# Transposes that load 104 stationary columns, and 104 partitions behind them, in a fused RWKV-7 and gated-cosine kernel

## The chip, the cores and the metric

The kernel runs on one core of a Trainium2 chip. The metric is the device time of one execution in microseconds (us); with one core, that core is the slowest. A profile shows one execution; the median is over several others.

The core's engines are TensorE (PE, with its weight loads listed apart as PEld), VectorE (DVE), ScalarE (ACT) and GpSimd (POOL). SyncE (SP) issues most of the DMAs. A matmul has two operands: the stationary one, which a weight load puts into the array, and the moving one, which streams past it. The stationary operand's columns become the output's partitions, the moving operand's columns become the output's columns.

## The reference

An attention block of the RWKV-7 kind runs a recurrence over 768 steps for 4 batches and 8 heads with head size 40. Its output feeds a feed-forward block with a cosine gate.

```python
for t in range(S):                                       # S = 768; r, k, v, w, a, b: (4, 8, 768, 40)
    y[:, :, t] = np.einsum('bhd,bhde->bhe', rt, state)
    Sa = np.einsum('bhde,bhe->bhd', state, at)
    state_decay = state * wt[:, :, None, :] - np.einsum('bhd,bhe->bhde', Sa, bt)
    state = state_decay + np.einsum('bhd,bhe->bhde', vt, kt)
x = y.transpose(0, 2, 1, 3).reshape(3072, 320)
h = x @ w_in                                             # w_in: (320, 2048)
out = (h * np.cos(h)) @ w_out                            # w_out: (2048, 320)
```

## The kernel before

**Tiling.** The sequence is cut into 24 chunks of C = 32 steps. A chunk of the 4 batches fills 128 partitions, as (batch, step). The 8 heads lie along the free dimension, each padded from D = 40 to DP = 64 columns, in tiles such as `nat`, `vp`, `rp`, `bn` and `kn`.

**Transposes.** Products within a chunk need head dimensions on partitions. `turned` (line 323) makes four transposes of a tile: each takes two neighbouring heads, 2 x 64 = 128 columns, as the stationary operand and the 128 x 128 identity as the moving one. In the result, partitions 0 to 39 hold the first head of the pair, 64 to 103 the second; 40 to 63 and 104 to 127 hold padding. `half` (line 76) names the two slices of 40 partitions that the later matmuls read. `full` (line 77) names the two halves of 64.

`turned` is called for the decays (`p1_w`), for a (`p1_a`), for b divided by a decay (`p1_b`), for v and r (`p2_v`) and for k (`p2_k`). Two places transpose on their own: `p1_a` turns the running decay products `wb` back to (batch, step) partitions for the first four chunks (line 415), and `ch_t` turns the state, eight transposes a chunk (line 558). After each group, ScalarE or VectorE copies the result out of PSUM. One PSUM tile of `at` is two banks, 2 x 512 columns of 128 partitions.

**What follows a transpose.** `p1_w` makes `wb`, the running products of decays within the chunk, by a scan on VectorE (chunks 0 to 3) or by a plain copy on ScalarE. `wc` keeps the last product of each chunk, and GpSimd sets the first one to 1 (`from_one`). `a_W` multiplies the turned a by `wb`. `p2_g`, `ch_q`, `ch_x` and `ch_s` are groups of small matmuls of 32 or 40 rows and columns. `ch_z` (line 629) accumulates the state's change in `dps`. It first zeroes whole halves of 64 partitions with a matmul of zeros. Then VectorE adds the change to the state `qz` (line 656), GpSimd multiplies the state by the chunk's decay `wc` (line 657), VectorE makes the outputs `yt` (line 663), and GpSimd scales these by `wb` (line 668). `tokens` sends two slices of 40 partitions of `yt` to DRAM and reads them back as `xT`.

**The feed-forward block.** It is cut into pieces: `first_a` and `first_b` make `ph` from `xT` and `w_in`, ScalarE and VectorE make the cosine gate, `second` makes `po`. `mm` (line 100) issues every matmul that isn't a transpose, so line 101 stands for all of them.

**Order.** The whole order is written out by hand: the scheduler is off, and for each chunk a list of segments (lines 919 to 994) says which piece of the recurrence and which piece of the feed-forward block comes next. Work that must come some steps later is put off with `later`. Each engine works through its list in this order. `busy` and `shifted` put extra matmuls of zeros at a few places.

Of the kernel before, what the change touches and what calls it, by code (L numbers as in the profile page):

```python
# [12 lines left out]
ALU = mybir.AluOpType  # L13
# [7 lines left out]
def kernel(  # L21
# [43 lines left out]
    nc = tc.nc  # L65
    B, H, S, D = r.shape
    P, C, DP = 128, 32, 64
# [4 lines left out]
    N72 = C + D  # L72
# [3 lines left out]
    half = [slice(DP * e, DP * e + D) for e in range(2)]  # L76
    full = [slice(DP * e, DP * e + DP) for e in range(2)]
    every = slice(0, P)

    const = ctx.enter_context(tc.tile_pool(name="const", bufs=1))  # L80
    ring = ctx.enter_context(tc.tile_pool(name="ring", bufs=7))
# [8 lines left out]
    def kept(name, shape, n=1, fill=None, part=lambda t: t, on=nc.gpsimd):  # L90

        tiles = []
        for i in range(n):
            t = const.tile(shape, F32, tag=f"{name}{i}", name=f"{name}{i}")
            if fill is not None:
                on.memset(part(t), fill)
            tiles.append(t)
        return tiles
# [4 lines left out]
    def pick(t, offset, *dims):  # L103

        return bass.AP(t.tensor, t.offset + offset, [list(t.ap[0]), *(list(d) for d in dims)])
# [8 lines left out]
    ident = kept("ident", [P, P])[0]  # L114
# [5 lines left out]
    for n, fill in (("w", 1.0), ("a", 0.0), ("b", 0.0)):  # L120
        for i in range(4):
            x = slice((i - 2) * H * DP, (i - 1) * H * DP)
            if i < 2:
                t = const.tile([P, H, DP], F32, tag=f"nat_{n}{i}", name=f"nat_{n}{i}")
            else:
                t = {
                    "w": w_in_sb[:, 0, late:], "a": w_in_sb[:, 1, late:], "b": late_out
                }[n][:, x].rearrange("p (h d) -> p h d", h=H)
# [4 lines left out]
    for n in "kvr":  # L133
        t = const.tile([P, H, D], F32, tag=f"nat_{n}", name=f"nat_{n}")
# [8 lines left out]
    NZ = 2 * (C + DP) - DP + D  # L143
    qz = kept("qz", [P, B, 2, NZ], 1, 0.0, on=nc.vector)[0]
# [178 lines left out]
    def turned(ps, x):  # L323

        for i in range(4):
            nc.tensor.transpose(  # L326
                ps[:, i * P : (i + 1) * P], x[:, 2 * i : 2 * i + 2].rearrange("p e d -> p (e d)"), ident
            )

    flat = lambda t: t.rearrange("p q t -> p (q t)")  # L330
    b4 = lambda t: t.rearrange("p (q t) -> p q t", t=C)
    unpad = lambda t: t[:, :, :D]
    G = {"rest": []}
# [24 lines left out]
    def p1_w(c):  # L358
        ps = at("wT")
        for i in range(2):  # L360
            turned(ps[:, i], nat["w", c + i])
        if c < 4:

            for i in range(2):
                nc.scalar.copy(G["w1"][:, i, :, 0:1], b4(ps[:, i])[:, :, 0:1])
            nc.vector.memset(ps[:, :, ::C], 0.0)
        for i in range(2):
            wb = ring.tile([P, 4 * P + 1], F32, tag="wb", name="wb")
            if c < 4:
                nc.vector.tensor_tensor_scan(  # L370
                    wb[:, 1:], ps[:, i], flat(G["w1"][:, i]), 0.0, ALU.mult, ALU.add
                )
            else:
                nc.scalar.copy(wb[:, 1:], ps[:, i])
            wc = ring.tile([P, 4 * B], F32, tag="wc", name="wc")
            nc.gpsimd.tensor_copy(wc, wb[:, C::C])
            G["wb", c + i], G["wx", c + i], G["wc", c + i] = wb, b4(wb[:, : 4 * P]), wc
            if c >= 4:
                from_one(c + i)
        if c == 8:  # L380
            later(2, lambda: over_w(c, unpad(nat["w", c])))
        elif c >= 4:
            over_w(c, unpad(nat["w", c]))

    def from_one(c):

        nc.gpsimd.memset(G["wb", c][:, : 4 * P : C], 1.0)

    def over_w(c, wn):
        rw = ring.tile([P, H, D], F32, tag="rw", name="rw")  # L390
# [4 lines left out]
    def a_W(c, aps):  # L395
        aT = ring.tile([P, 4, P], F32, tag="aT", name="aT")
        nc.vector.tensor_tensor(
            aT.rearrange("p j (b t) -> p (j b) t", b=B), b4(aps), G["wx", c], ALU.mult
        )
        G["aT", c] = aT  # L400

    def p1_a(c):
        if c >= 4:
            ps = at("aps")
            for i in range(2):
                turned(ps[:, i], nat["a", c + i])
            for i in range(2):
                a_W(c + i, ps[:, i])
            over_w(c + 1, unpad(nat["w", c + 1]))
            return  # L410
        for c in range(c, c + 2):
            wn = ps_h.tile([P, 512], F32, tag="h", name="wn")
            aps = ps_o.tile([P, 512], F32, tag="o", name="aps")
            for j in range(4):
                nc.tensor.transpose(
                    wn[:, j * P : (j + 1) * P], G["wb", c][:, j * P + 1 : (j + 1) * P + 1], ident
                )
            from_one(c)
            turned(aps, nat["a", c])
            over_w(c, unpad(wn.rearrange("p (h d) -> p h d", h=H)))  # L420
            a_W(c, aps)

    def p1_b(c):
        ps = at("bT")
        for i in range(2):
            turned(ps[:, i], bn_b[(c + i) % 7])
        for i in range(2):
            bT = sb3.tile([P, 4, P], F32, tag="opT", name="bT")
            nc.scalar.copy(bT.rearrange("p j t -> p (j t)"), ps[:, i])
            G["bT", c + i] = bT  # L430

    def p1_n(c):
# [75 lines left out]
    def p2_v(c):  # L508
        ps = at("vT")
        turned(ps[:, 0], vp)  # L510
        turned(ps[:, 1], rp)
        G["vT"] = sb3.tile([P, 4, P], F32, tag="opT", name="vT")
        G["rT", c] = sb2.tile([P, 4, P], F32, tag="rT", name="rT")
        nc.scalar.copy(G["vT"].rearrange("p j t -> p (j t)"), ps[:, 0])
        nc.scalar.copy(G["rT", c].rearrange("p j t -> p (j t)"), ps[:, 1])

    def p2_k(c):
        ps = at("kT")
        turned(ps[:, 0], kn_b[c % 2])
        G["kT"] = sb3.tile([P, 4, P], F32, tag="opT", name="kT")  # L520
        nc.scalar.copy(G["kT"].rearrange("p j t -> p (j t)"), ps[:, 0])

    def p2_g(c):
        kT, vT, aT, rT = G["kT"], G["vT"], G["aT", c], G["rT", c]
# [29 lines left out]
    def ch_t(c):  # L554
        ps = at("sT")
        G["s"] = sb1.tile([P, 2 * B, P], F32, tag="s", name="s")
        for i in range(2 * B):
            nc.tensor.transpose(  # L558
                ps[:, i // 4, (i % 4) * P : (i % 4 + 1) * P], qz[:, i // 2, i % 2, C : C + P], ident
            )  # L560
        for i in range(2):
            nc.scalar.copy(G["s"][:, 4 * i : 4 * i + 4].rearrange("p i e -> p (i e)"), ps[:, i])  # L562

    def ch_q(c):
        ps = at("qps")
# [63 lines left out]
    def ch_z(c):  # L629
        ps = [at("dps") for _ in range(2)]  # L630
        sm = G["sm"]

        for bb in range(B):
            for e in range(2):
                mm(
                    ps[bb // 2][full[e], bb % 2, : 4 * N72], idle[blk[bb], :DP],
                    pick(idle[blk[bb]], 0, (0, 4), (1, N72)), True,
                )
        for s, n in ((0, kn_b[c % 2]), (1, bn_b[c % 7])):
            for j in range(4):  # L640
                o = C - C * (j // 2)
                for bb in range(B):
                    for e in range(2):
                        mm(
                            ps[bb // 2][half[e], bb % 2, j * N72 : (j + 1) * N72],
                            n[blk[bb], 2 * j + e, :D],
                            sm[e][blk[bb], j, :] if s else vvm[c % 2][blk[bb], 2 * j + e, o : o + N72],
                            False,
                        )
        wx, wc = G["wx", c], G["wc", c]  # L650
        yt = sb1.tile([P, 4, B, C], F32, tag="yt", name="yt")
        for bb in range(B):
            dp = ps[bb // 2][:, bb % 2]
            if c < NCH - 1:
                z = pick(qz[:, bb], C, (DP, 2), (NZ, 2), (1, D))
                nc.vector.tensor_tensor(z, pick(dp, 0, (2 * N72 + C, 2), (N72, 2), (1, D)), z, ALU.add)  # L656
                nc.gpsimd.tensor_tensor(  # L657
                    z, z,
                    wc.rearrange("p (f m b) -> p f m b", f=2, m=2)[:, :, :, bb]
                    .unsqueeze(3).to_broadcast([P, 2, 2, D]),  # L660
                    ALU.mult,
                )
            nc.vector.tensor_tensor(  # L663
                yt.rearrange("p (f m) b t -> p f m b t", f=2)[:, :, :, bb],
                pick(dp, D, (2 * N72 - D, 2), (N72, 2), (1, C)),
                pick(qz[:, bb], 0, (NZ - C, 2), (NZ, 2), (1, C)), ALU.add,
            )
        nc.gpsimd.tensor_tensor(  # L668
            yt.rearrange("p j b t -> p (j b) t"), yt.rearrange("p j b t -> p (j b) t"), wx, ALU.mult
        )  # L670
        later(2, lambda: tokens(c, yt))

# [158 lines left out]
    with tc.manual_schedule():  # L831
# [88 lines left out]
        for c in range(NCH):  # L920
            t, q, x, s, z = main(c)
# [109 lines left out]
```

## Time and profile before

| | |
|---|---|
| runs before, us | 825.33, 826.02, 822.83; median 825.33 |
| the profiled execution, span from first to last instruction | 823.7 us; the profile gives no other time for it |
| mean granted TensorE clock | 0.948 of full |
| TensorE busy from 240 to 760 us | 515.25 of 520.00 us, clock 1.00 |
| TensorE busy from 0 to 62 us | 31.88 us, clock 0.76 |
| transposes of line 326: matmuls, weight loads | 88.13 us, 70.53 us, 576 of each |
| transposes of line 558: matmuls, weight loads | 26.4 us, 21.7 us, 184 of each |
| transposes of line 415: matmuls, weight loads | 4.3 us, 3.2 us, 16 of each |

Busy times of matmuls and loads overlap, with each other and among themselves: a matmul is counted from its start to its modelled end, and the next may start before that. So a mean duration isn't the distance from one matmul to the next; the distance comes from how long a group of several takes. A group's row in the profile gives line, engine, operation, output<-inputs, shapes, count, busy us, mean ns of one, and the engine's idle time before it with what ended it. A shape such as 128*128 128x320 is the rows and columns of the stationary operand, then those of the moving one.

### The profile page before, as it was taken

What the parts mean: (1) busy time and instruction counts of PE and PEld (TensorE: products, weight loads), DVE (VectorE), ACT (ScalarE), POOL (GpSimd) and SP (SyncE); (2) the same over time, 40 slices, a digit from 0 to 9 for tenths busy, and PEclk for the clock granted to TensorE, in tenths of its full rate; (3) what the DMA queues carried; (4) which work ended last, traced back from release to release, by engine and by line L of the source; (5) the groups of instructions that cost most, each with busy time, mean ns of one, the idle gap of its engine ahead of it and who ended that gap; (6) DMA issues with size and microseconds to landing.
All of it is one profiled execution on the core that took longest, in us unless ns stands there. A gap on an engine that the chain in (4) does not pass through costs nothing.

```text
span 823.7 us, 37673 instructions
## 1 busy us (share of the span) xinstructions
PE 746.9 (91%) x16832; PEld 571.3 (69%) x16832; DVE 509.3 (62%) x1081; ACT 383.8 (47%) x707; POOL 201.3 (24%) x352
## 2 busy tenths in 40 slices
PE   3656778899689999999999999999999999999997
PEld 2534456677467777778777777777787777777775
DVE  6987887859645599354797553895444874332231
ACT  1214676544244553545446446435635445363352
POOL 5315554430214023212221230330330222201000
PEclk9757799899789999999999999999999999999999
DMA  8456663244043322333223323214310212101000
GB/s 120 78 132 168 173 162 104 46 119 69 25 98 84 64 59 52 69 100 65 54 37 71 68 63 67 61 37 65 66 41 24 45 35 52 21 21 37 20 17 16
DMA packets 183297, 55.66 MB, mean 68 GB/s; under 512 B 157152, under 2 KB 178656, under 8 KB 183136
## 3 DMA queue, kind: packets, MB, share of 16 engines
q1 hardware_dynamic: 180560, 51.95, 29.2%
q8 instruction: 132, 2.16, 1.1%
q10 hardware_dynamic: 2320, 0.98, 0.6%
q0 software_dynamic: 256, 0.33, 0.2%
q14 instruction: 29, 0.24, 0.1%
HBM read 42.07 MB, written 11.14 MB: 65 GB/s over the span
## 4 chain that ended last, share of the span: by engine, by line
PE 63%; DVE 19%; ACT 6%; DMA 4%; issue 3%; SPq 3%; POOL 1%; DVEq 0%; ACTq 0%; POOLq 0%
PE ph L101 22%; PE po L101 20%; DVE inv_tmp L468 4%; DVE inv L472 4%; PE x0ps L101 3%; PE dps L101 3%; SPq L152 3%; PE gram L101 2%; DVE rw L391 2%; PE vT L326 2%; PE sps L101 2%; PE qps L101 1%; DVE turns L732 1%; PE nps L101 1%; PE sT L558 1%
## 5 line engine op out<-in xcount | busy, mean ns | idle before, releaser
L101 PE MATMUL po<-w_out_sb,gT 128*128 128x320 f32 x768 | 227.0, 445 | 0.0
L101 PE MATMUL ph<-xT,w_in_sb 128*128 128x256 f32 x768 | 189.5, 393 | 4.8 <-DVE gT L740 3.8
L101 PEld LDWEIGHTS po<-w_out_sb,gT 128*128 128x128 f32 x768 | 142.4, 193 | 55.9 <-issue 4.2
L101 PEld LDWEIGHTS ph<-xT,w_in_sb 128*128 128x128 f32 x768 | 142.3, 194 | 33.9 <-issue 13.9
L730 ACT ACTIVATE turns<-ph,rnd 128x512 f32<-128x512 f32 x96 | 63.8, 685 | 157.2 <-PE ph L101 156.7
L732 DVE SCALAR_TENSOR_TENSOR turns<-turns,ph 128x512 f32<-128x512 f32 x96 | 63.8, 684 | 109.2 <-ACT turns L730 108.9
L740 DVE TENSOR_TENSOR gT<-ph,turns 128x512 f32<-128x512 f32 x96 | 65.6, 685 | 36.3 <-ACT turns L737 36.3
L657 POOL TENSOR_TENSOR qz<-qz,wc 128x160 f32<-128x160 f32 x92 | 43.2, 489 | 163.1 <-DVE qz L656 162.6
L472 DVE TENSOR_TENSOR inv<-inv,inv_tmp 128x31 f32<-128x31 f32 (+15 forms) x186 | 72.0, 387 | 6.4
L468 DVE TENSOR_TENSOR inv_tmp<-u,inv 128x31 f32<-128x31 f32 (+15 forms) x186 | 70.0, 376 | 4.4
L736 ACT ACTIVATE turns<-turns 128x512 f32<-128x512 f32 x96 | 60.2, 627 | 23.3 <-DVE turns L732 23.3
L737 ACT ACTIVATE turns<-turns,half_pi 128x512 f32<-128x512 f32 x96 | 69.3, 722 | 3.1
L490 POOL COPY vp<-nat_v 128x320 f32<-128x320 f32 x25 | 12.5, 501 | 182.9 <-DMA nat_v<-in_v_dram 144.1
L101 PE MATMUL ph<-xT,w_in_tail 64*128 64x256 f32 x384 | 54.8, 404 | 0.0
L656 DVE TENSOR_TENSOR qz<-dps,qz 128x160 f32<-128x160 f32 x92 | 28.9, 315 | 33.9 <-PE dps L101 33.8
L391 DVE RECIPROCAL rw<-nat_w 128x320 f32<-128x320 f32 x20 | 42.8, 2142 | 0.1
L562 ACT COPY s<-sT 128x512 f32<-128x512 f32 x46 | 24.5, 584 | 37.6 <-PE sT L558 37.6
L101 PEld LDWEIGHTS ph<-xT,w_in_tail 64*128 64x128 f32 x384 | 33.3, 187 | 10.4 <-issue 6.6
L668 POOL TENSOR_TENSOR yt<-yt,wb 128x512 f32<-128x512 f32 x24 | 31.3, 1306 | 22.4 <-DVE yt L663 22.4
L546 ACT COPY vvm<-gram 128x256 f32<-128x256 f32 x24 | 8.8, 368 | 55.6 <-DVE ag L541 55.3
L101 PEld LDWEIGHTS sps<-x,rt 32*32 32x32 f32 x1536 | 18.1, 109 | 21.6 <-issue 16.5
L101 PE MATMUL sps<-x,rt 32*32 32x72 f32 x1536 | 23.0, 240 | 10.7 <-DVE rt L476 9.0
(118 smaller groups left out, 1070.1 us busy)
## 6 DMA issues: line engine op xcount, KB each, us to landing
words<-in_moe_w_in_dram SPq DMA_DIRECT2D x8, 512.0 KB
nat_k<-in_k_dram SPq DMA_DIRECT2D x96, 40.0 KB
nat_v<-in_v_dram SPq DMA_DIRECT2D x96, 40.0 KB
nat_r<-in_r_dram SPq DMA_DIRECT2D x96, 40.0 KB
xd<-yt SPq DMA_DIRECT2D x48, 80.0 KB
out_dram<-ot SPq DMA_DIRECT2D x24, 160.0 KB
nat_b<-in_b_dram SPq DMA_DIRECT2D x88, 40.0 KB
wd<-ws SPq DMA_DIRECT2D x5, 640.0 KB
```

The source lines that it names most:

```text
L101: nc.tensor.matmul(o, lhsT=lhsT, rhs=rhs, start=start, stop=stop, skip_group_check=True)
L391: nc.vector.reciprocal(rw, wn)
L468: nc.vector.tensor_tensor(tmp, u[:, j : j + 1, :j].to_broadcast([P, C - j, j]), x[:, j:, j : j + 1].to_broadcast([P, C - j, j]), ALU.mult,)
L472: nc.vector.tensor_tensor(x[:, j:, :j], x[:, j:, :j], tmp, ALU.subtract)
L656: nc.vector.tensor_tensor(z, pick(dp, 0, (2 * N72 + C, 2), (N72, 2), (1, D)), z, ALU.add)
L657: nc.gpsimd.tensor_tensor(z, z, wc.rearrange("p (f m b) -> p f m b", f=2, m=2)[:, :, :, bb] .unsqueeze(3).to_broadcast([P, 2, 2, D]), ALU. ...
L668: nc.gpsimd.tensor_tensor(yt.rearrange("p j b t -> p (j b) t"), yt.rearrange("p j b t -> p (j b) t"), wx, ALU.mult)
L730: nc.scalar.activation(n, u, ACTF.Identity, bias=rnd, scale=1.0)
L732: nc.vector.scalar_tensor_tensor(n, n, -ROUND, u, ALU.add, ALU.subtract)
L736: nc.scalar.activation(n, n, ACTF.Abs)
L737: nc.scalar.activation(n, n, ACTF.Sin, bias=half_pi, scale=-2.0 * math.pi)
L740: nc.vector.tensor_tensor(gT[:, 2 * e : 2 * e + 2].rearrange("p f t -> p (f t)"), us[e], ns[e], ALU.mult)
```

## The change

A new slice `live` names the partitions 0 to 103 (DR = 64 + 40). The transposes of `turned` and `ch_t` take 104 stationary columns instead of 128, and so write 104 partitions. The transposes of line 415 contract over 104 rows, with a 104 x 104 part of the identity as the moving operand. Every copy, scan, product and memset between these transposes and their readers works on partitions 0 to 103. Tiles keep their sizes. The last 24 partitions of those tiles are not written, and nothing reads them.

```diff
+    DR = DP + D
+    live = slice(0, DR)
...
             nc.tensor.transpose(
-                ps[:, i * P : (i + 1) * P], x[:, 2 * i : 2 * i + 2].rearrange("p e d -> p (e d)"), ident
+                ps[live, i * P : (i + 1) * P],
+                x[:, 2 * i : 2 * i + 2].rearrange("p e d -> p (e d)")[:, live], ident,
             )
...
-                nc.scalar.copy(G["w1"][:, i, :, 0:1], b4(ps[:, i])[:, :, 0:1])
-            nc.vector.memset(ps[:, :, ::C], 0.0)
+                nc.scalar.copy(G["w1"][live, i, :, 0:1], b4(ps[live, i])[:, :, 0:1])
+            nc.vector.memset(ps[live, :, ::C], 0.0)
...
-                    wb[:, 1:], ps[:, i], flat(G["w1"][:, i]), 0.0, ALU.mult, ALU.add
+                    wb[live, 1:], ps[live, i], flat(G["w1"][live, i]), 0.0, ALU.mult, ALU.add
...
-                nc.scalar.copy(wb[:, 1:], ps[:, i])
+                nc.scalar.copy(wb[live, 1:], ps[live, i])
...
-            nc.gpsimd.tensor_copy(wc, wb[:, C::C])
+            nc.gpsimd.tensor_copy(wc[live], wb[live, C::C])
...
-        nc.gpsimd.memset(G["wb", c][:, : 4 * P : C], 1.0)
+        nc.gpsimd.memset(G["wb", c][live, : 4 * P : C], 1.0)
...
-            aT.rearrange("p j (b t) -> p (j b) t", b=B), b4(aps), G["wx", c], ALU.mult
+            aT[live].rearrange("p j (b t) -> p (j b) t", b=B), b4(aps[live]), G["wx", c][live], ALU.mult
...
-                    wn[:, j * P : (j + 1) * P], G["wb", c][:, j * P + 1 : (j + 1) * P + 1], ident
+                    wn[:, j * P : j * P + DR], G["wb", c][live, j * P + 1 : (j + 1) * P + 1], ident[live, live]
...
-            nc.scalar.copy(bT.rearrange("p j t -> p (j t)"), ps[:, i])
+            nc.scalar.copy(bT[live].rearrange("p j t -> p (j t)"), ps[live, i])
...
-                ps[:, i // 4, (i % 4) * P : (i % 4 + 1) * P], qz[:, i // 2, i % 2, C : C + P], ident
+                ps[live, i // 4, (i % 4) * P : (i % 4 + 1) * P], qz[:, i // 2, i % 2, C : C + DR], ident
...
-                z = pick(qz[:, bb], C, (DP, 2), (NZ, 2), (1, D))
-                nc.vector.tensor_tensor(z, pick(dp, 0, (2 * N72 + C, 2), (N72, 2), (1, D)), z, ALU.add)
+                z = pick(qz[live, bb], C, (DP, 2), (NZ, 2), (1, D))
+                nc.vector.tensor_tensor(z, pick(dp[live], 0, (2 * N72 + C, 2), (N72, 2), (1, D)), z, ALU.add)
                 nc.gpsimd.tensor_tensor(
                     z, z,
-                    wc.rearrange("p (f m b) -> p f m b", f=2, m=2)[:, :, :, bb]
-                    .unsqueeze(3).to_broadcast([P, 2, 2, D]),
+                    wc[live].rearrange("p (f m b) -> p f m b", f=2, m=2)[:, :, :, bb]
+                    .unsqueeze(3).to_broadcast([DR, 2, 2, D]),
                     ALU.mult,
                 )
```

The copies of v, r, k and the state (`p2_v`, `p2_k`, `ch_t`) and the two products that make `yt` (lines 663 and 668) change in the same way.

## The prediction

> **What bounds the kernel now.** I read the page first: engine shares, the slices with the granted clock, the chain that ended last.
>
> ```profile
> span 823.7 us, 37673 instructions
> PE 746.9 (91%) x16832; PEld 571.3 (69%) x16832; DVE 509.3 (62%) x1081; ACT 383.8 (47%) x707; POOL 201.3 (24%) x352
> PEclk9757799899789999999999999999999999999999
> PE 63%; DVE 19%; ACT 6%; DMA 4%; issue 3%; SPq 3%; POOL 1%; DVEq 0%; ACTq 0%; POOLq 0%
> ```
>
> TensorE sets the end from about 240 us on, where it is busy nearly without a break at full clock; before that, loads, VectorE and a lower clock share the chain. The largest parts of the chain are the two MoE products `ph` and `po` (22% and 20%), which the change leaves alone. The question is what a transpose costs on TensorE, and which of its two halves, weight load (PEld) or matmul (PE), sets that cost. So next I read the groups with shapes kept apart (busy us, mean ns of one, idle before).
>
> ```profile
> L101 PEld LDWEIGHTS ph<-xT,w_in_sb 128*128 128x128 f32 x768 | 142.3, 194 | 33.9 <-issue 13.9 <-DMA xT<-xd 1.3
> L574 ACT COPY qz<-qps 40x512 f32<-40x512 f32 x46 | 26.6, 578 | 6.1 <-PE qps L101 5.7
> L562 ACT COPY s<-sT 128x512 f32<-128x512 f32 x46 | 24.5, 584 | 37.6 <-PE sT L558 37.6
> L101 PE MATMUL pad<-idle 128*1 128x1 bf16 x186 | 5.1, 163 | 2.5 <-issue 2.5
> L101 PEld LDWEIGHTS <-idle 128*1 128x1 bf16 x186 | 4.8, 81 | 3.1 <-issue 2.6 <-DVE inv_tmp L468 0.4
> L194 POOL TENSOR_SCALAR_AFFINE_SELECT su<-su 32x128 f32<-32x128 f32 x4 | 1.2, 302 | 0.1
> masks.py:199 POOL TENSOR_SCALAR_AFFINE_SELECT ident<-ident 128x128 f32<-128x128 f32 x1 | 0.3, 283 | 0.0
> ```
>
> Then two groups of transposes in the timeline of the dense part: eight state transposes at 409.7 us and eight of the decays at 412.4 us.
>
> ```profile
> 409.74 1.06 PEld L558 LDWEIGHTS sT<-ident,qz 128*128 128x128 f32 x8
> 410.00 1.04 PE L558 MATMUL sT<-ident,qz 128*128 128x128 f32 x8
> ...
> 412.39 1.01 PEld L326 LDWEIGHTS wT<-ident,nat_w 128*128 128x128 f32 x8
> 412.61 1.04 PE L326 MATMUL wT<-ident,nat_w 128*128 128x128 f32 x8
> ```
>
> One such matmul lasts 273 ns and one load 140 ns (medians of both lines). Eight matmuls in 1.04 us mean a start every (1040 - 273) / 7 = 110 ns. The same sum for the `ph` products, 8 in 1.89 us at 382 ns each, gives a start every 215 ns for 256 moving columns: twice the columns, twice the step, though both have 128 stationary columns. The step follows the moving columns. The load of a transpose starts while the matmul before it runs (the first at 409.74, where the last `po` matmul starts, 0.26 us ahead of its own matmul), and 140 ns of load fit a 110 ns step because loads overlap too. Transposes are matmul-bound, at the 128 columns of the identity.
>
> **What the Trainium skill says.** "TensorE: Matmul & The Clock Gate", section "LDWEIGHTS (loading the stationary operand)": the load's time goes with its columns (P / 1.2 ns), not its rows; for 128 columns 107 ns, for 104 columns 87 ns. Here a transpose's load costs less: where it has no cover, the next matmul is about 55 ns late (328 instead of 273 ns for the first matmul of such a group), so I scale 55 ns instead, and get 10 ns for 24 columns. The same page, "Step-by-step: what each phase is for", says that the next tile's weights load while this tile's matmul runs; the timeline agrees. Its section "Weight-path perf modes" ties a fast weight load to exactly 128 weights and a type other than FP32: the transposes are f32, yet their load (140 ns) is 50 ns shorter than that of the f32 products (about 190 ns), so I can't exclude that some fast path needs 128. "VectorE: DVE Perf Modes", section "Why `tensor_reduce` can't reduce along partition axis", calls each of the 128 partitions an independent pipeline; for VectorE no row before has fewer partitions to show it.
>
> **The change, part by part.** Instructions, their order and their waits are the same on every engine; only extents shrink. Nothing is moved, no DMA changes.
>
> 1. Stationary columns, lines 326 and 558, 576 + 184 = 760 transposes; line 415 keeps 128 stationary columns. Moving columns stay 128, so the 110 ns step stays. A load saves 10 ns (half clock: 20), hidden wherever the load lies under the matmul before. Pairing all 776 transposing matmuls with their loads in the trace, 53 start within 20 ns of their load and 15 more, at half clock, 30 to 35 ns after it: only these 68 feel the load. 53 x 10 + 15 x 20 = 0.83 us if all are on the chain. Cover for the other 708 is the preceding matmul; without it, they would save 7 to 14 us.
>
> 2. The `wn` transposes, line 415, 16, all in the first 25 us at half clock: moving columns fall from 128 to 104, the step from 213 to 173 ns: 16 x 40 = 0.64 us. The reciprocals of line 391 (2.15 us each on VectorE) come after them, waited for `wn` only 0.2 us, and VectorE is the fuller engine there. I count a third: 0.2 us; bounds 0 and 0.64.
>
> 3. Copies out of PSUM and products on 104 partitions. ScalarE: lines 374, 429, 514, 515, 521 and 562, some 90 us, at 574 to 594 ns for 512 elements. A 40-partition copy of 512 elements takes 578 ns beside 584 ns for 128 partitions: nothing gained or lost. GpSimd: lines 376, 387, 657, 668, 5.6 + 3.2 + 43.2 + 31.3 = 83 us; 32 partitions take 302 ns and 128 take 283 ns in the select above, so fewer partitions gain nothing, and may cost up to the 7% between those two; PE would see only the part after line 657 (bounds 0 and 0.07 x 13.0 us of its waits for line 657 = 0.9 us; I take 0). VectorE: lines 366, 370, 397, 656, 663, about 75 us; I take no change, by the independent lanes. Should 2% of it come off or on, that is 1.5 us, the range's business.
>
> Sum: -0.83 x 0.7 (PE's share of the chain is 63%, more where the exposed loads lie) - 0.2 = -0.8 us against the span of 823.7. The median of the runs, 825.33, stands 1.6 us above the span; what lies around is untouched, so 824.5.
>
> **Rivals.**
>
> *The short load is slower per column.* If a fast path needs 128 columns, 104 columns cost the f32 rate: the products' load is 50 ns longer for 128 columns, so about 105 for 128 and 85 for 104, against 55 now. Still under the 110 ns step, so hidden loads stay hidden; 68 exposed ones lose 30 ns: +2 us, 827.4. For: the gap of 140 to 190 ns. [...]
>
> *The load is no longer taken ahead* (the slower side). If a load short of 128 columns waits for the matmul in flight, each of the 708 hidden loads shows its 45 ns: 708 x 45 = 32 us, 857. It decides once 4.1 us show, so at 92 such loads. Against: the one-column pads load 128 rows x 1 column, and 75 of them stand in the chain with 1.94 us, 26 ns each, although one load lasts 81 and one matmul 163 ns: partial loads are taken ahead. But that is another column group, not 104 of 128.
>
> *Engines pay for 104 partitions.* [...]104 might take another branch. The state product of line 657 is what the state transposes wait for (5.4 + 7.6 us in nine waits). Some ten exposed chunks x 4 products need +100 ns of 489 each for 4.1 us; then about 830. In the dense part there is slack: at 408.3 us the last product ends, at 409.7 the first state load starts.
>
> *The matmul shortens too.* If the step followed the stationary columns, 110 would become 90: 760 x 20 = 15 us, at 63% on the chain -9.6 us, 815. Against: `ph` and transposes differ only in moving columns, and their steps are as 2 to 1; and x0ps with 32 stationary columns still lasts 231 ns for 72 moving ones.
>
> **How the numbers follow.** Hidden loads 0.77, slower per column 0.08, not taken ahead 0.05, engines 0.05, matmul shortens 0.05. The three runs before lie 3.2 us apart (822.83 to 826.02), and a shift of nanoseconds can re-order arrivals, so the likeliest case has +-2.5 us of its own: 822.0 to 827.0. With the slow-load case the range is 821.8 to 828.2. A measurement of this kernel can tell about 0.5% (4.1 us) from no change: faster means under 821.2, slower over 829.5. Faster 0.08 (matmul case and the low tail), same 0.79 (likeliest and slow load), slower 0.13 (the two other rivals and the upper tail).
>
> **What would show it.** Right: the state-transpose group still 1.04 us for eight, its load 130 ns, `wn` matmuls near 380 instead of 421 ns, copies within 1% of 584 ns, line 657 near 489 ns. A load of about 170 ns is the slow-load rival; eight matmuls in about 1.35 us is the load not taken ahead; 0.90 us is the matmul case; line 657 near 600 ns is the engine rival. The prediction is wrong if the step of 110 ns moves, or if anything but extents differs in the rows.

## The result: 0.3% slower

The changed kernel takes 826.13 us in the median of 17 runs (822.87 to 829.32). The kernel before takes 822.83 us in the median of 17 (820.99 to 827.11); the three of them on which the prediction rests, with a median of 825.33, had lain high. The ratio is 1.003, with a 95% interval of 1.0014 to 1.0046: 1.2 to 3.8 us slower. The forecast was 824.5 us and no change, with 0.8 us gained. The time is inside the range, and the ratio is below the 0.5% that counts as a change here, but the interval lies wholly on the slower side. One execution of a later run, 1275.55 us at a granted clock of 0.80, is left out of its ratio.

Below are the head of the page, one group of copies, the `wn` matmuls and two groups of transposes (from the page, the groups with shapes kept apart and the timeline, all of the changed kernel), as answers to the lines of before.

```profile
span 823.6 us, 37673 instructions
PE 742.0 (90%) x16832; PEld 565.8 (69%) x16832; DVE 512.4 (62%) x1081; ACT 384.7 (47%) x707; POOL 202.8 (25%) x352
PE 61%; DVE 22%; ACT 5%; DMA 4%; issue 4%; SPq 2%; POOL 1%; DVEq 0%; ACTq 0%; POOLq 0%
```

```profile
L565 ACT COPY s<-sT 104x512 f32<-104x512 f32 x46 | 24.5, 585 | 37.5 <-PE sT L561 37.5
L418 PE MATMUL wn<-ident,wb 104*128 104x104 f32 x16 | 3.7, 386 | 3.7 <-DVE wb L373 3.7
```

The `wn` matmuls of before, for comparison:

```profile
L415 PE MATMUL wn<-ident,wb 128*128 128x128 f32 x16 | 4.3, 426 | 3.7 <-DVE wb L370 3.7
```

The transposes of the changed kernel:

```profile
408.10 1.05 PEld L561 LDWEIGHTS sT<-ident,qz 128*104 128x104 f32 x8
408.36 1.04 PE L561 MATMUL sT<-ident,qz 128*104 128x128 f32 x8
...
410.75 1.00 PEld L328 LDWEIGHTS wT<-ident,nat_w 128*104 128x104 f32 x8
410.96 1.04 PE L328 MATMUL wT<-ident,nat_w 128*104 128x128 f32 x8
```

On TensorE all is as forecast. Eight transposes still take 1.04 us, so a start every 110 ns. The median load fell from 141 to 130 ns (forecast 130), the `wn` matmuls from a mean of 426 to 386 ns (forecast near 380), and the copies stay at 585 ns. Where a transpose's load has no cover, the matmul after it fell from 328 to 318 ns (medians), the 10 ns of the sum. So three rivals are out: their signs were a load of about 170 ns, eight matmuls in 1.35 us, and eight in 0.90 us. TensorE is busy 4.9 us less in sum. The chain shows where to look instead: VectorE's share rose from 19% to 22%, and VectorE is busy 3.1 us longer (509.3 to 512.4) with the same instructions.

The two profiled executions are equally long (823.7 and 823.6 us), because that of before was one of its slower ones. So the loss isn't the difference of these two spans; it has to be found place by place.

**Where VectorE's time grew.** With the two traces beside each other, instruction by instruction, few VectorE instructions differ by over 0.1 us from 240 us on, and the large differences stand where the inverse (lines 468 and 472; 471 and 475 in the changed kernel) meets GpSimd's end of the state update: in chunks 7, 11 and 19. This is the timeline of chunk 7 before, VectorE and GpSimd:

```profile
312.68 0.36 DVE L468 TENSOR_TENSOR inv_tmp<-u,inv 128x207 f32<-128x207 f32 x1
313.07 0.52 DVE L472 TENSOR_TENSOR inv<-inv,inv_tmp 128x207 f32<-128x207 f32 x1
313.32 1.39 POOL L668 TENSOR_TENSOR yt<-yt,wb 128x512 f32<-128x512 f32 x1
313.63 1.30 DVE L468 TENSOR_TENSOR inv_tmp<-u,inv 128x192 f32<-128x192 f32 x1
314.67 0.98 POOL L497 TENSOR_TENSOR kn<-nat_k,rw 128x320 f32<-128x320 f32 x1
314.96 0.90 DVE L472 TENSOR_TENSOR inv<-inv,inv_tmp 128x192 f32<-128x192 f32 x1
```

And the same instructions of the changed kernel:

```profile
310.74 1.09 POOL L660 TENSOR_TENSOR qz<-qz,wc 104x160 f32<-104x160 f32 x2
...
311.14 0.37 DVE L471 TENSOR_TENSOR inv_tmp<-u,inv 128x207 f32<-128x207 f32 x1
311.55 1.74 DVE L475 TENSOR_TENSOR inv<-inv,inv_tmp 128x207 f32<-128x207 f32 x1
311.79 1.26 POOL L671 TENSOR_TENSOR yt<-yt,wb 104x512 f32<-104x512 f32 x1
313.02 0.99 POOL L500 TENSOR_TENSOR kn<-nat_k,rw 128x320 f32<-128x320 f32 x1
313.32 0.90 DVE L471 TENSOR_TENSOR inv_tmp<-u,inv 128x192 f32<-128x192 f32 x1
314.25 0.49 DVE L475 TENSOR_TENSOR inv<-inv,inv_tmp 128x192 f32<-128x192 f32 x1
```

Before, the two engines take turns. GpSimd's last state product ends, VectorE's waiting inverse step gets through (0.52 us), GpSimd's `yt` product has to wait for it (1.39 us instead of 1.27), and VectorE's next step waits for that (1.30 us). After, VectorE's step began 0.25 us ahead of the `yt` product in the same way, but is passed over, which here means that the other engine's next instruction gets through while it still waits: it lasts 1.74 us and ends 0.23 us after the `yt` product. The three steps take 0.52 + 1.30 + 0.90 = 2.72 us before and 1.74 + 0.90 + 0.49 = 3.13 us after. VectorE is 0.41 us later from there on, and TensorE waits for it at the next transposes of v, 10 us later. The lines are from the timelines of before and after:

```profile
323.38 0.63 PE L326 MATMUL vT<-ident,vp 128*128 128x128 f32 x4 [0.51 <-DVE vvm L547]
```

```profile
322.27 0.61 PE L328 MATMUL vT<-ident,vp 128*104 128x128 f32 x4 [0.96 <-DVE vvm L550]
```

The wait grew from 0.51 to 0.96 us. Chunk 11 is the same; in chunk 19 the delay doesn't reach TensorE. Chunk 1, with VectorE at the weights' conversion, has a larger case. The timeline of before, and then that of after:

```profile
102.95 1.06 POOL L657 TENSOR_TENSOR qz<-qz,wc 128x160 f32<-128x160 f32 x2
103.00 0.69 DVE L241 TENSOR_SCALAR mant<-words 128x512 int32<-128x512 int32 x1
103.62 0.68 DVE L242 TENSOR_SCALAR expo<-words 128x512 int32<-128x512 int32 x1
103.98 1.45 POOL L668 TENSOR_TENSOR yt<-yt,wb 128x512 f32<-128x512 f32 x1
```

```profile
103.04 3.36 POOL L660 TENSOR_TENSOR qz<-qz,wc 104x160 f32<-104x160 f32 x2
...
106.25 3.03 DVE L259 TENSOR_TENSOR w_in_sb<-mant,expo 128x512 f32<-128x512 f32 x1 [0.18 <-ACT mant L256]
106.36 1.26 POOL L671 TENSOR_TENSOR yt<-yt,wb 104x512 f32<-104x512 f32 x1
106.45 0.18 PEld L561 LDWEIGHTS sT<-ident,qz 128*104 128x104 f32 x2 [2.01 <-POOL qz L660]
```

Here GpSimd is the one passed over: its last two state products take 3.36 us together instead of 1.06, while VectorE passes six conversion instructions (103.45 to 106.08 us), and the next chunk's state transposes wait 2.01 us for it. Then GpSimd passes two, and VectorE's next instruction takes 3.03 us.

The Trainium skill, "SBUF — State Buffer", section "SBUF: two separate sides", says that VectorE and GpSimd share a pair of ports, that the one which starts first holds it for a whole instruction (of VectorE's, those with two inputs in SBUF, as the inverse steps have, or in a two-port mode), and that the other fully blocks. The blocking is what these lines show: 1.39 us instead of 1.27 for a `yt` product that waits. Starting first isn't enough in them, though: VectorE's step began 0.25 us ahead of the `yt` product and ended 0.23 us after it.

### The profile page after: what moved, and what is told of

Same layout as the page of the kernel before. It is cut to its first block, busy times and chain, and to the rows that moved or that the text cites. A ratio compares the mean times of both kernels' runs of the same rounds, so it can differ in the third digit from the quotient of the medians.

```text
span 823.6 us, 37673 instructions
## 1 busy us (share of the span) xinstructions
PE 742.0 (90%) x16832; PEld 565.8 (69%) x16832; DVE 512.4 (62%) x1081; ACT 384.7 (47%) x707; POOL 202.8 (25%) x352
## 4 chain that ended last, share of the span: by engine, by line
PE 61%; DVE 22%; ACT 5%; DMA 4%; issue 4%; SPq 2%; POOL 1%; DVEq 0%; ACTq 0%; POOLq 0%
PE ph L103 22%; PE po L103 19%; DVE inv L475 5%; DVE inv_tmp L471 5%; PE x0ps L103 3%; PE dps L103 3%; DVE rw L394 3%; PE gram L103 2%; PE sps L103 2%; SPq L154 2%; PE vT L328 2%; PE nps L103 2%; PE qps L103 1%; DMA ws<-in_w_dram 1%; DVE turns L735 1%
## 5 line engine op out<-in xcount | busy, mean ns | idle before, releaser
L103 PE MATMUL ph<-xT,w_in_sb 128*128 128x256 f32 x768 | 187.0, 389 | 6.1 <-DVE gT L743 3.7
L103 PEld LDWEIGHTS ph<-xT,w_in_sb 128*128 128x128 f32 x768 | 140.6, 192 | 35.2 <-issue 15.9
L660 POOL TENSOR_TENSOR qz<-qz,wc 104x160 f32<-104x160 f32 x92 | 46.1, 520 | 160.3 <-DVE qz L659 159.8
L475 DVE TENSOR_TENSOR inv<-inv,inv_tmp 128x31 f32<-128x31 f32 (+15 forms) x186 | 75.1, 404 | 6.4
L659 DVE TENSOR_TENSOR qz<-dps,qz 104x160 f32<-104x160 f32 x92 | 29.1, 316 | 34.0 <-PE dps L103 33.9
L565 ACT COPY s<-sT 104x512 f32<-104x512 f32 x46 | 24.5, 585 | 37.5 <-PE sT L561 37.5
L671 POOL TENSOR_TENSOR yt<-yt,wb 104x512 f32<-104x512 f32 x24 | 30.6, 1276 | 22.4 <-DVE yt L666 22.4
```

The costliest lines, as they stand in the source:

```text
L103: nc.tensor.matmul(o, lhsT=lhsT, rhs=rhs, start=start, stop=stop, skip_group_check=True)
L475: nc.vector.tensor_tensor(x[:, j:, :j], x[:, j:, :j], tmp, ALU.subtract)
L659: nc.vector.tensor_tensor(z, pick(dp[live], 0, (2 * N72 + C, 2), (N72, 2), (1, D)), z, ALU.add)
L660: nc.gpsimd.tensor_tensor(z, z, wc[live].rearrange("p (f m b) -> p f m b", f=2, m=2)[:, :, :, bb] .unsqueeze(3).to_broadcast([DR, 2, 2, D] ...
L671: nc.gpsimd.tensor_tensor(yt[live].rearrange("p j b t -> p (j b) t"), yt[live].rearrange("p j b t -> p (j b) t"), wx[live], ALU.mult)
```

## The experiments

Three theories. **A**: the state update's instructions on 104 partitions cost it, through the turns of VectorE and GpSimd. **B**: the shorter loads shift TensorE by nanoseconds, and that redraws how the engines meet. **C**: nothing systematic; such meetings fall anew in every execution.

### Both kernels once more

No edit.

> The kernel before, unchanged, against itself: what two sets of runs of one program differ by. Theory A (the change costs 0.3% through the pairing of VectorE and GpSimd instructions after the state update: where a GpSimd yt product begins 0.25 us after an inverse step of VectorE, one of two outcomes follows, with VectorE 2.7 or 3.1 us for three steps): ratio 1.000 within 0.0015; and the outcome with 1.39 us for the yt product at 313, 431, 547 and 667 us as in the first profile of before. Theory C (nothing systematic: the outcome is drawn anew in each execution, and the 0.3% are such draws and the early stage): the outcomes at these four places differ from the first profile of before in at least one, and the ratio may lie 0.0015 to 0.003 off 1.

> The changed kernel once more. Theory A: ratio 1.0015 to 1.0045, and the yt product takes 1.26 us at 312, 429 and 667 us again, with an inverse step of 1.74 us beside it. Theory C: ratio between 0.999 and 1.002, and the outcomes at these places differ from the first profile of the changed kernel.

Before against itself: 0.9994 (0.9978 to 1.001). The changed kernel: 1.0044 (1.0022 to 1.0065). The turns of chunks 7, 11, 15 and 19 repeat exactly: the `yt` product takes 1.39 to 1.40 us at all four places in both profiles of before; in both profiles of after it takes about 1.27 us in chunks 7, 11 and 19, with an inverse step of 1.73 to 1.75 us beside it, and 1.40 us in chunk 15. C falls for these places. In chunk 1 the second profile of after has 0.64 us, not 2.9: that place does vary. But there VectorE's next instruction takes 3.68 us, against 1.76 us for the longest one in both profiles of before.

### The transposes alone, and the state update alone

The first keeps the decays and the state update on 128 partitions; its core:

```diff
-    def turned(ps, x):
+    def turned(ps, x, live=live):
...
-            turned(ps[:, i], nat["w", c + i])
+            turned(ps[:, i], nat["w", c + i], every)
```

with `live` in `turned`, `a_W`, `p1_b`, `p2_v`, `p2_k` and `ch_t` as in the change, and lines 365 to 387, 415 and `ch_z` as before. The second has the change in `ch_z` alone (lines 655 to 669).

> Only the transposes of a, b, v, r, k and of the state load 104 columns, with their copies and the a product on 104 partitions; the decays and the whole state update stay on 128. Theory A: ratio 1.000 within 0.0015, since GpSimd and VectorE instructions of the state update are those of before. Theory B (shorter loads shift TensorE by some ns at 68 places, and the shift alone makes the later collisions fall otherwise): 1.002 to 1.004. Theory C: between 0.998 and 1.002.

> Only the four kinds of instructions of the state update (two on VectorE, two on GpSimd) work on 104 partitions; all transposes load 128 columns. Theory A: 1.0015 to 1.0045, with the yt product at 1.26 us and an inverse step of 1.74 us at 312, 430 and 667 us. Theory B: 1.000 within 0.0015. Theory C: between 0.998 and 1.002. By the rows of the profile the GpSimd state product stays at 460 ns and VectorE's sum at 310 to 316 ns where nothing collides.

Transposes alone: 0.9984 (0.9967 to 1.0), all four places with 1.40 us. State update alone: 1.003 (1.0017 to 1.0043), all of the loss, with 1.27 us and a step of 1.74 to 1.75 us in chunks 7, 11 and 19 and a product of 2.91 us in chunk 1. B falls, A stands. The transposes alone give -1.3 us (-2.7 to 0). The sum had -0.6 us for the loads, with those of the decays, which this run leaves at 128; the interval holds that, and reaches no change at its end.

### Which of the four instructions

Theories from here: **G**, the partition count of the GpSimd instruction that VectorE meets; **V**, VectorE's own two instructions; **P**, any shift of some ns. For the state product alone:

```diff
                 nc.gpsimd.tensor_tensor(
-                    z, z,
-                    wc.rearrange("p (f m b) -> p f m b", f=2, m=2)[:, :, :, bb]
-                    .unsqueeze(3).to_broadcast([P, 2, 2, D]),
+                    pick(qz[live, bb], C, (DP, 2), (NZ, 2), (1, D)), pick(qz[live, bb], C, (DP, 2), (NZ, 2), (1, D)),
+                    wc[live].rearrange("p (f m b) -> p f m b", f=2, m=2)[:, :, :, bb]
+                    .unsqueeze(3).to_broadcast([DR, 2, 2, D]),
```

The other two have `live` in line 668 alone, or in lines 655 and 656 alone with the product of line 657 on 128.

> Only GpSimd's state product (line 657 of the kernel before) works on 104 partitions. Theory G (the partition count of the GpSimd instruction that meets VectorE's instructions decides who gets through): the fourth product of chunk 1, at about 101 to 103 us, takes 2.9 us instead of 0.64, some 2 us are lost there (ratio 1.002 to 1.003), and the four yt products near 310, 427, 545 and 665 us take 1.39 us as before. Theory V (VectorE's two instructions decide): nothing changes, chunk 1 has 0.64 us, ratio 1.000 within 0.0015. Theory P (any shift of a few ns redraws the outcomes): a mixture that fits neither.

> Only GpSimd's product for yt (line 668 of the kernel before) works on 104 partitions. Theory G: 1.26 us for it at three of the four places near 310, 427 and 665 us, with an inverse step of VectorE of 1.74 us beside each, 0.4 us lost twice (ratio 1.0005 to 1.0015); chunk 1 keeps 0.64 us for the fourth state product. Theory V: 1.39 us at all four, ratio 1.000 within 0.0015. Theory P: a mixture that fits neither.

> Only VectorE's state sum (line 656 of the kernel before) works on 104 partitions. Theory G: everything as before, 0.64 us in chunk 1 and 1.39 us at the four places, ratio 1.000 within 0.0015. Theory V: 2.9 us in chunk 1 or 1.26 us at three of the places, ratio 1.001 to 1.003. Theory P: a mixture.

The state product alone gives 1.0104 (1.0059 to 1.0148, from four runs), more than the whole change and more than any theory had. The other two show the turns of before at all four places (1.39 to 1.40 us): the `yt` product alone 1.0015 (1.0001 to 1.003), the state sum alone 1.001 (0.9994 to 1.0027). So it is the state product that changes the turns. The interval of the `yt` product just excludes 1; a small loss that the turns don't show isn't ruled out there. V falls for the state sum; VectorE's `yt` sum was not tried alone, but has 104 with the others in the last kernel below. G is right about the kind of instruction and wrong about the places and the size: it took the `yt` product as the one that matters at the four. What goes wrong there begins with the state product before it. The timeline of chunk 7 with the state product alone on 104:

```profile
310.93 1.09 POOL L659 TENSOR_TENSOR qz<-qz,wc 104x160 f32<-104x160 f32 x2
...
311.74 2.56 DVE L474 TENSOR_TENSOR inv<-inv,inv_tmp 128x207 f32<-128x207 f32 x1
311.99 1.27 POOL L670 TENSOR_TENSOR yt<-yt,wb 128x512 f32<-128x512 f32 x1
313.22 0.85 POOL L499 TENSOR_TENSOR kn<-nat_k,rw 128x320 f32<-128x320 f32 x1
```

VectorE's step is passed over twice, by the `yt` and by the `kn` product: 2.56 to 2.57 us, now in chunks 7, 11, 15 and 19, and TensorE waits about 1.2 us instead of 0.5 at the v transposes in three of them. In chunk 1 the product itself takes 0.68 us, but a VectorE instruction beside it takes 1.92 us.

There are four more such places, in chunks 6, 10, 14 and 18, where VectorE's step comes during the `yt` product and waits for that one alone: 1.34 to 1.37 us in every other profile of the kernel, with 104 partitions in all four instructions too. With the state product alone on 104 it takes 2.56 to 2.57 us in all four. Chunk 6 in the timelines of before and of this kernel:

```profile
291.20 1.34 DVE L468 TENSOR_TENSOR inv_tmp<-u,inv 128x207 f32<-128x207 f32 x1
```

```profile
289.17 2.56 DVE L470 TENSOR_TENSOR inv_tmp<-u,inv 128x207 f32<-128x207 f32 x1
```

From there TensorE waits 0.74 to 0.97 us for `x` in chunks 7, 11 and 15, at most 0.40 us in the other profiles.

### How many partitions

The state update on 120 instead of 104, and the whole change with 112 and with 120. Each is one constant: `DR = 120` or `DR = 112` in place of `DR = DP + D`. E and H are named in the expectations.

> The four instructions of the state update work on 120 partitions instead of 104, so that every group of 16 partitions has some. Theory G in the form that a whole group of 16 partitions without work matters: as with 128, 0.64 us in chunk 1 and 1.39 us at the four places, ratio 1.000 within 0.0015. Theory G in the form that any count short of 128 matters: as with 104, 2.9 us in chunk 1, 1.26 us at three of four places, ratio 1.0015 to 1.0045. Theory P: a mixture.

> The whole change with one constant set otherwise: 112 stationary columns and 112 partitions instead of 104. The last 16 partitions have no work, as with 104. Theory E (a GpSimd instruction that leaves a whole group of 16 partitions without work upsets the turn-taking with VectorE): ratio 1.0015 to 1.0045, and 1.26 us for the yt product at two or more of the four places near 312, 429, 547 and 667 us, with inverse steps of 1.7 us or more. Theory H (104 is no multiple of 16, and that matters): as with 128, 1.39 us at all four, ratio 0.998 to 1.000.

> The whole change with 120 stationary columns and partitions: all eight groups of 16 partitions have work, the last one half. Theory E: 1.39 us for the yt product at all four places, at most 0.9 us for the fourth state product of chunk 1, ratio 0.997 to 1.000, since the slightly shorter loads are all that is left of the change. Theory H: as with 104, ratio 1.0015 to 1.0045.

With 120 the state update gives 1.0002 (0.9982 to 1.0022) and the whole change 0.9993 (0.9977 to 1.001), with 1.39 to 1.40 us at all four places. With 112 the whole change gives 1.0017 (0.9994 to 1.004), with 1.26 to 1.28 us and steps of 1.74 to 1.75 us in chunks 7, 11 and 19, 1.39 us in chunk 15, and 2.91 us in chunk 1: the turns of 104. The ratio's interval for 112 still holds 1, so by time alone this one isn't settled; by the turns it is, and H, which had 112 as 128 and 120 as 104, falls. Over all profiles of the whole kernel, the seven with 120 or 128 partitions in the state product have no step passed over in chunks 7, 11, 15 and 19, 28 of 28; the five with 104 or 112 have one in 16 of 20, and the four without are all chunk 15 where the `yt` product too has fewer partitions. In chunk 1 the longest VectorE instruction lasts 1.75 to 1.76 us in all seven; in the five it lasts 3.03 us (three times), 3.68 us, and 1.92 us with the state product alone. That VectorE starts some nanoseconds earlier or later isn't what decides at the four places, so P falls there: the inverse step ahead (line 468) begins 23 to 55 ns before the last state product in the first group and 26 to 55 ns in the second.

### The meeting by itself

> Computes nothing of the reference: fourteen sections in which 16 VectorE products of 128 x 256 elements meet ten GpSimd products of p x 160 elements, with p = 128, 120, 112, 104, 96, 64, then one product on 104 (and one on 120) ahead of nine on 128, then the first six sections again. VectorE and GpSimd are independent within a section. Theory E: with 128 and 120 the two engines take turns, no VectorE product lasting more than 1.0 us; with 112, 104 and 96, and perhaps 64, single VectorE products or single GpSimd products last 1.5 us or more, since one engine passes several of its instructions while the other waits. Theory H: 120 behaves as 104, and 112, 96 and 64 as 128. If all sections look alike, the meeting of these two kinds of products isn't what upsets the turns.

All fourteen sections take turns alike, whatever the count; the longest VectorE product lasts 0.79 us, with 64. Theory E fails as put there: fewer partitions in GpSimd's products alone don't upset the turns. The next kernel keeps the shapes and the order of the state update:

> Computes nothing of the reference. Each of 24 sections holds one state update as the kernel has it (four times VectorE's state sum, GpSimd's state product and VectorE's yt sum, then GpSimd's yt product and its k product) followed by sixteen VectorE instructions of the inverse, with these partitions for the four: 128, 120, 112, 104 for all; 104 for the state product alone; 96 and 64 for all; 104 for all but the state product; and the whole list three times. Theory E (a state product with a group of 16 partitions without work, met by VectorE, upsets the turns after it): no VectorE instruction over 1.5 us in the sections with 128 and 120 and where the state product alone has 128; one of 1.7 us or more in the sections with 112, 104, 96 and 64, and one of 2.5 us where the state product alone has 104. Theory F (more of the kernel is needed: an arrival of TensorE's results or DMA traffic): all sections alike, as in the earlier kernel of this kind.

Its timeline, first a section with 120 for all, then one with 104, then one with 104 in the state product alone:

```profile
21.10 0.39 DVE L54 TENSOR_TENSOR inv_tmp<-u,inv 128x231 f32<-128x231 f32 x1
21.52 0.54 DVE L58 TENSOR_TENSOR inv<-inv,inv_tmp 128x231 f32<-128x231 f32 x1
21.77 1.41 POOL L86 TENSOR_TENSOR yt<-yt,wb 120x512 f32<-120x512 f32 x1
22.10 1.33 DVE L54 TENSOR_TENSOR inv_tmp<-u,inv 128x220 f32<-128x220 f32 x1
...
40.07 0.39 DVE L54 TENSOR_TENSOR inv_tmp<-u,inv 128x231 f32<-128x231 f32 x1
40.49 1.76 DVE L58 TENSOR_TENSOR inv<-inv,inv_tmp 128x231 f32<-128x231 f32 x1
40.74 1.25 POOL L86 TENSOR_TENSOR yt<-yt,wb 104x512 f32<-104x512 f32 x1
42.28 0.92 DVE L54 TENSOR_TENSOR inv_tmp<-u,inv 128x220 f32<-128x220 f32 x1
...
50.10 2.58 DVE L58 TENSOR_TENSOR inv<-inv,inv_tmp 128x231 f32<-128x231 f32 x1
50.35 1.26 POOL L86 TENSOR_TENSOR yt<-yt,wb 128x512 f32<-128x512 f32 x1
51.57 0.85 POOL L87 TENSOR_TENSOR kn<-kn,k 128x320 f32<-128x320 f32 x1
```

These are the three pictures of the kernel, without TensorE and without DMA traffic: F falls, and E's forecast holds in 23 of the 24 sections. Each kind of section stands three times in the one execution. The longest VectorE instruction of a section:

| partitions | three sections, us |
|---|---|
| 128 for all | 1.33, 1.34, 1.34 |
| 120 for all | 1.33, 1.33, 1.33 |
| 112 for all | 1.76, 1.76, 1.33 |
| 104 for all | 1.76, 1.76, 1.76 |
| 96 for all | 1.76, 1.76, 1.76 |
| 64 for all | 1.76, 1.76, 1.76 |
| 104 in the state product alone | 2.58, 2.58, 2.58 |
| 104 in all but the state product | 1.33, 1.33, 1.33 |

From the state sum's start to the end of the inverse steps a section takes 9.35 to 9.51 us in the turn-taking ones, 9.63 to 9.70 us with one step passed over, and 9.91 to 9.92 us with two.

## Why the prediction was wrong

**Right: parts 1 and 2, and the copies of part 3.** Load, step, `wn` and copies came out as forecast, and the transposes alone gave -1.3 us (-2.7 to 0) where the sum had -0.6 for the loads.

**Wrong: part 3, GpSimd.** The step took the state product of line 657 at no cost, with a bound of 0.9 us from a 7% longer instruction. The instruction isn't longer: 460 ns before and 462 ns after (medians); the mean rose from 489 to 520 ns by two single ones of 1.70 and 2.92 us that had to wait. Its cost is who gets through after it: with 104 partitions in the state update the kernel is 0.3% slower (1.003), with 120 it isn't (1.0002). The failure was to price an instruction by its own row only, and to look for no price in what meets it. The profile of before had the signs: inverse steps with a mean of 387 ns and single ones of 1.3 us beside a `yt` product of 1.39 us instead of 1.27.

**The engine rival** named the right instruction and the right waiter (line 657, the state transposes) and looked for the price in its duration, +100 ns in each of some 40. Nothing of that kind shows. The cover that it counted on in the dense part, 1.4 us between the last product and the first state load, held; VectorE's inverse steps went another way round, to `vvm` and from there to the v transposes. That 826.13 us lies inside the forecast range is luck: the range's width stood for scatter and for a slower load, and the loss came by a path that the sum didn't have.

**What the 2.5 us are made of.** Two waits of TensorE at the v transposes, in chunks 7 and 11, are 0.95 to 0.96 us in every profile with 104 or 112 partitions in the whole state update, and 0.51 to 0.56 us in those with 120 or 128: 2 x 0.41 = 0.8 us. The rest lies in the first two chunks. The second `yt` product starts at 102.0 to 104.0 us in the seven profiles with 120 or 128 (mean 103.0) and at 104.3, 105.4, 106.4 and 106.6 us in the four with 104 or 112 in the whole update (mean 105.7). That is 2.6 us, with a scatter of about 1 us; at the fourth `yt` product 1.9 us of it are left (173.7 and 175.5 us in the mean). Three of the four have the product of 2.9 us in chunk 1, and the fourth a VectorE instruction of 3.68 us. The sum, 1.9 + 0.8 = 2.7 us, fits the ratio (1.2 to 3.8 us) and the spans, 2.3 us longer in the mean, but its early part rests on four executions in a stretch that varies anyway.

**What stays open.** Why chunks 6, 10, 14, 15 and 18 are spared when all four instructions have 104 or 112, why one of three sections with 112 took turns, and why products of one size against one another take turns at any count. The runs show when it happens, not by what rule the next turn is given. Whether a group of 16 partitions without work is what matters isn't shown either: the counts that were tried leave any boundary between 112 and 120. The state product alone lost some 8.6 us by its ratio, from four runs. From the `yt` product of chunk 6 on its profile is 4.6 us longer than the middle of the others; the longer waits for `x` and at the v transposes make about 4 us of that. The rest of the 8.6 us, in the early part, wasn't followed further.

**No version beats both.** The whole change on 120 partitions (0.9993) keeps the turns of before, and the transposes alone (0.9984, interval up to 1.0) the shorter loads; neither is clear of no change.

## What to carry to other kernels

Where the start of one transpose after another is set by the matmul, as here with a start every 110 ns before and after, a narrower stationary operand saves only where a load has no cover, here 68 of 776. When a GpSimd instruction that runs against VectorE is cut to fewer partitions, look at the VectorE instructions beside it: the price can stand in their rows, not in its own. In this kernel 120 partitions kept the turns and 112 did not. For an edit that costs nothing by durations, list the single instructions whose time is a multiple of their mean and ask what they meet.

## What was not expected of the hardware

A GpSimd state product on 112, 104, 96 or 64 partitions, met by VectorE, can let a VectorE instruction be passed over by the next GpSimd instruction, 1.76 us instead of 0.54 (in all sections but one with 112); on 128 or 120 it never did. With the other three instructions on 128 it is passed over twice, 2.58 us. The count makes no difference to the instruction itself: 460 ns for 160 elements on 104, 120 and 128 partitions, where nothing meets it.
